# Fused attention and two MoE layers: the beginning split over three DMA queues

## The chip, the cores and the metric

One Trainium2 chip, one of its NeuronCores. The metric is the device time of the program in microseconds, on the slowest core (here the only one); the number given is the median of several executions. Lower is better.

## What is computed

Inputs are float32: q, k and v of 4 batches, 12 heads, 448 positions and 64 channels; two 12 x 12 matrices that mix heads; the weights of two feed-forward layers.

```python
scores = scale * np.matmul(q, k.transpose(0, 1, 3, 2))
scores = np.einsum('bhij,hg->bgij', scores, w_pre)
scores = scores - np.max(scores, axis=-1, keepdims=True)
attn = np.exp(scores)
attn = attn / (np.sum(attn, axis=-1, keepdims=True) + 1e-09)
attn = np.einsum('bhij,hg->bgij', attn, w_post)
x = np.matmul(attn, v)               # then (4*448) x 768 tokens
h = x @ w_in                         # 768 -> 2048, a piecewise quadratic gate, @ w_out
y = softmax-weighted h, layer norm   # 768 -> 1024, * g_ln, @ w_out2
```

## The kernel before, in words

**Order.** The program is not written in the order in which it runs. Every step is a task of a planner (`Order`, L66): an engine, an estimated duration, a priority, the tasks it depends on, and the buffer rings it takes from. `emit` (L100) plays the tasks through on estimated clocks, on each engine always the one that can start first and of those the one with the smallest priority number, and then emits the instructions in that order. So an instruction's place in its engine's queue is fixed by the priorities in `OFFS` (L27) and by estimated durations; on the chip each engine then works through its queue in order and waits where a semaphore tells it to. A DMA is two tasks: the issue, on the engine that issues it, and the transfer, on one estimated DMA server. GpSimd issues through the software queue (q0 in the page), SyncE through the hardware queue (q1).

**Attention.** Work goes through 16 chunks (4 batches x 4 parts of 110 or 118 query rows). A chunk has six qk tasks (`qk`, L297), one for two heads: four 64-row matmuls into two PSUM tiles of the ring `psa` (4 tiles). Each head's scores are evicted to an SBUF tile of the ring `s` (12 tiles; `qk_evac`, L311), on ScalarE, but in the first chunk the odd heads on VectorE. Then a DMA (`remap`, L320) puts them into `sr`: a tile in which a partition is one head and one of ten rows, so that heads lie side by side for mixing. There are two `sr` tiles, used in turn by chunks. Remaps are issued by SyncE, those of the first chunk's odd heads by GpSimd. When all 12 remaps of a chunk have landed, `pre` (L326) mixes heads by matmuls with `wp`, for two tiles of queries at a time (a pair; 90 pairs in all). `rmax` (L335), `expo` (L340), `guard`, `norm` and `wscale` make the softmax and fold its divisor into the second mixing matrix; `post` (L360) mixes again and turns; `evac` (L383) puts the result into `at`, and `av` (L397) multiplies with v. Results go to memory and from there into the two feed-forward layers (`moe`), which run on TensorE until the end.

**The beginning.** `zero_w` (L239) is one GpSimd task: memsets of `wb`, `mk`, `qb`'s padding, `wp` and a strip of `at`. `load_w` (L249), also GpSimd, issues eight small DMAs: the mask four times and the two mixing matrices twice each. `make_w` (L257) multiplies matrices and mask into `wp` and `wk` on VectorE. `zero_s` (L246) sets the four unused rows of each `sr` tile to zero with a VectorE memset, one at the start, one after the first chunk's last eviction (L552). The first chunk's k and q are loaded by SyncE in the pieces listed in `start` (L29): k0, q of pair 0, k1, q of pairs 1 and 2, k2 and k3, q of pairs 3 to 5, k4 and k5 (L524 to L532). The q of every later chunk is one task of two DMAs (L534), whose priority is `sq` below its chunk's first tile; the list `gates` makes such a load wait for a pre matmul where its slot is not negative (L570).

Of the kernel before, what the change touches and what calls it, by code (L numbers as in the profile page):

```python
# [20 lines left out]
HR = 5  # L21
# [5 lines left out]
OFFS = dict(split=-29.45, pre=-0.17, rmax=7.13, expo=-13.24, guard=20.77, norm=-7.75, post=5.7, eh=-57.18, el=-77.04, av0=7.24, avs=1.89, sq=-28.23, exact=174, sld=1000, linact=(), wral=0, early=17, b_in=1000.28, b_x=928.04, b_out=999.37, b_x1=973.79, lw=-90, shal=147, wrp=(), vlp=(),  # L27
   qk0=-14.58, qks=0.45, dmalat=2100, sk=-12.53, sv=3.3, nv=1, svs=0.59,
   mw=-5, start=(('k', 0, 1), ('q', 0, 1), ('k', 1, 1), ('q', 1, 2), ('k', 2, 2), ('q', 3, 3), ('k', 4, 2)))  # L29
# [188 lines left out]
def attention(nc, od, pl, q, k, v, w_pre, w_post, mask, xs):  # L218
# [20 lines left out]
    def zero_w():  # L239
        nc.gpsimd.memset(wb, 0.0)  # L240
        nc.gpsimd.memset(mk, 0.0)
        nc.gpsimd.memset(qb[:, :, :QPAD], 0.0)
        nc.gpsimd.memset(wp, 0.0)
        nc.gpsimd.memset(at[:, :, :, 2 * SEG - R:2 * SEG].rearrange('p k h c -> p (k h) c'), 0.0)

    def zero_s(i):  # L246
        nc.vector.memset(sr[i][0:pad], 0.0)

    def load_w():  # L249
        for i in range(2):  # L250
            for j, w in enumerate((w_pre, w_post)):
                o = 64 * i + (0 if i or j else pad)
                rows = slice(o, o + HR * H)
                nc.gpsimd.dma_start(out=mk[rows, j], in_=mask[:HR, :HR].unsqueeze(1).to_broadcast([HR, H, HR]))
                nc.gpsimd.dma_start(out=wb[rows, j], in_=w.unsqueeze(0).to_broadcast([HR, H, H]))
# [17 lines left out]
    def load_k(b, p):  # L273
        t = pl['kraw'].tile([128, S], F32, tag="kraw", name="kraw")
        nc.sync.dma_start(out=t, in_=k[b, p])
# [180 lines left out]
    t_zs = [add("DVE", 5700, -120, zero_s, 0)]  # L456
    t_lw = add("Pool", 8000, P['lw'], load_w, deps=[t_z], lat=2500)
    t_w = add("DVE", 300, P['mw'], make_w, deps=[t_lw])
# [25 lines left out]
    def make_two(two):  # L484
# [13 lines left out]
        for g, (b, k, pa, pb) in enumerate(groups):  # L498
# [3 lines left out]
            for r in range(2):  # L502
# [3 lines left out]
                    deps=[m] + avs.get(n - 3, []), use=[(r_psb, -2 + r)]))  # L506
# [12 lines left out]
    for i, (b, c) in enumerate(chunks):  # L519
        t0 = t  # L520
        n = GR[c] * R
        if i == 0:
            q0 = {}
            for what, h0, nh in P['start']:  # L524
                if what == 'k':
                    for p in range(h0, h0 + nh):
                        kt[b, p] = od.dma("SP", 450, 640, -100, load_k, b, p, new=[r_kraw])
                else:
                    a1 = od.dma("SP", 1250, nh * 400, -100, load_q, i, b, c, h0, nh,
# [3 lines left out]
        else:  # L533
            a1 = od.dma("SP", 1250, 2000, t0 + P['sq'] - 3, load_q, i, b, c, 0, H // 2, new=[r_q])  # L534
# [588 lines left out]
```

## Time and profile before

| | us |
|---|---|
| median of 3 executions | 1099.97 |
| lowest, highest | 1094.51, 1102.66 |
| the profiled execution | 1098.48 |
| its span, first to last instruction | 1096.7 |
| TensorE busy in it | 1045.8 |
| VectorE, ScalarE, GpSimd busy | 645.6, 553.4, 333.9 |

The profile is of one execution. Busy time is the union of an engine's instructions; on TensorE, where matmuls overlap, a busy stretch is not one at its peak. DMA share is the mean busy share of the core's 16 DMA engines; it can be over 1, since packets overlap. The granted clock is a share of TensorE's full speed.

### The profile page before, as it was taken

The numbers are of one execution on the slowest core, as the hardware profiler recorded it, in microseconds if no ns is written. First come the engines' busy times: TensorE is split into PE (matmuls) and PEld (weight loads), VectorE is DVE, ScalarE is ACT, GpSimd is POOL, SyncE is SP. The second block draws the span as 40 slices with busy tenths as digits, with TensorE's granted clock in tenths as the row PEclk, the third lists the DMA queues.
The fourth block names the chain that finished last, engine by engine and source line by source line (L and its number), as shares of the span: only waits on it lengthen the run. The fifth ranks groups of instructions, "written<-read, shape, count | busy, mean of one in ns | idle before, by whom it ended". The sixth has DMA issues, their size and how long they took to land.

```text
span 1096.7 us, 26955 instructions
## 1 busy us (share of the span) xinstructions
PE 1045.8 (95%) x11200; PEld 866.0 (79%) x11200; DVE 645.6 (59%) x1091; ACT 553.4 (50%) x1201; POOL 333.9 (30%) x438
## 2 busy tenths in 40 slices
PE   6979999999897799999999999999999999999998
PEld 1546666656564699989899998989998899898998
DVE  4445555556457773686869687878766533442242
ACT  3768887788676466433434343343453322333222
POOL 3111111111117854454545455656311000000000
PEclk9999999999999899999999999999999999999999
DMA  8774774775744451423322242424123000000001
GB/s 180 214 198 137 222 213 144 211 225 161 218 149 161 126 181 49 130 81 94 127 82 103 99 142 72 144 101 144 53 79 99 1 30 15 29 15 29 29 15 44
DMA packets 78858, 124.71 MB, mean 114 GB/s; under 512 B 20673, under 2 KB 65825, under 8 KB 78737
## 3 DMA queue, kind: packets, MB, share of 16 engines
q1 hardware_dynamic: 78000, 121.79, 36.7%
q0 software_dynamic: 736, 1.21, 0.6%
q8 instruction: 88, 1.44, 0.6%
q14 instruction: 34, 0.27, 0.1%
HBM read 66.96 MB, written 17.30 MB: 77 GB/s over the span
## 4 chain that ended last, share of the span: by engine, by line
PE 77%; DVE 10%; DMA 4%; ACT 3%; POOL 3%; issue 3%; SPq 0%; ACTq 0%; POOLq 0%; DVEq 0%
PE ps_pre L333 6%; PE ps_h L747 6%; PE ps_h L749 6%; PE ps_h L748 6%; PE ps_o L777 5%; PE ps_o L779 5%; PE ps_qk L306 5%; PE ps_o L778 5%; PE ps_av L420 5%; PE ps_post L369 5%; PE ps_ot L1004 4%; PE ps_ot L1005 4%; PE ps_ot L1003 4%; PE ps_h L943 4%; PE ps_h L945 4%; PE ps_h L944 3%
## 5 line engine op out<-in xcount | busy, mean ns | idle before, releaser
L777 PE MATMUL ps_o<-g,wout 128*128 128x448 f32 x384 | 139.9, 364 | 5.2 <-DVE x2acc L787 5.2
L779 PE MATMUL ps_o<-g,wout 128*128 128x448 f32 x384 | 139.2, 362 | 0.0
L778 PE MATMUL ps_o<-g,wout 128*128 128x448 f32 x384 | 138.8, 362 | 0.0
L369 PEld LDWEIGHTS ps_post<-wr,p 64*64 64x64 f32 x5040 | 101.4, 136 | 47.3 <-issue 29.5
L338 DVE TENSOR_REDUCE nm<-ps_pre 128x1 f32<-128x448 f32 x180 | 105.2, 618 | 48.0 <-PE ps_pre L333 43.7
L343 ACT ACTIVATE p<-ps_pre,nm 128x448 f32<-128x448 f32 x180 | 115.0, 649 | 30.7 <-DVE nm L338 30.6
L666 POOL TENSOR_TENSOR m<-m,v 128x768 f32<-128x768 f32 (+1 forms) x52 | 93.2, 1792 | 80.2 <-DVE v L648 39.5
L787 DVE TENSOR_TENSOR x2acc<-ps_o,x2acc 128x448 f32<-128x448 f32 x168 | 100.4, 617 | 28.1 <-PE ps_o L779 27.8
L369 PE MATMUL ps_post<-wr,p 64*64 64x60 f32 x5040 | 102.0, 221 | 11.3 <-issue 5.5
L769 POOL TENSOR_TENSOR g<-t,g 128x448 fp32r<-128x448 f32 x64 | 89.3, 1399 | 76.4 <-ACT g L765 75.5
L306 PE MATMUL ps_qk<-kraw,qb 64*64 64x448 f32 (+2 forms) x768 | 102.0, 565 | 10.1 <-DMA qb<-in_q_dram 5.3
L333 PE MATMUL ps_pre<-sr,wp 64*64 64x448 f32 (+1 forms) x720 | 99.3, 563 | 9.1 <-DVE at L391 3.5
L317 ACT ACTIVATE s<-ps_qk 119x448 f32<-119x448 f32 (+1 forms) x186 | 92.4, 577 | 29.5 <-PE ps_qk L306 22.1
L350 POOL TENSOR_SCALAR nm<-nm 128x2 f32<-128x2 f32 x90 | 19.1, 212 | 226.4 <-ACT p L343 225.9
L777 PEld LDWEIGHTS ps_o<-g,wout 128*128 128x128 f32 x384 | 72.0, 187 | 13.0 <-DVE x2acc L787 8.6
L638 ACT ACTIVATE v<-v,ebias 128x768 int32<-128x768 int32 (+1 forms) x52 | 46.0, 884 | 66.5 <-DVE v L634 63.2
L779 PEld LDWEIGHTS ps_o<-g,wout 128*128 128x128 f32 x384 | 72.0, 188 | 4.9
L778 PEld LDWEIGHTS ps_o<-g,wout 128*128 128x128 f32 x384 | 72.0, 187 | 4.9
L420 PE MATMUL ps_av<-at,vv 128*64 128x240 f32 (+1 forms) x648 | 72.1, 364 | 3.5 <-issue 3.5
L657 POOL TENSOR_SCALAR m<-m 128x768 f32<-128x768 f32 (+1 forms) x52 | 48.6, 935 | 85.9 <-DVE m L642 59.4
L949 DVE TENSOR_REDUCE st<-ps_h 128x1 f32<-128x1024 f32 x14 | 17.1, 1225 | 96.5 <-PE ps_h L945 96.5
L753 ACT ACTIVATE t<-ps_h,half 128x448 f32<-128x448 f32 x64 | 40.2, 629 | 62.1 <-PE ps_h L749 60.7
(121 smaller groups left out, 2332.2 us busy)
## 6 DMA issues: line engine op xcount, KB each, us to landing
sr<-s SPq DMA_DIRECT2D x138, 192.5 KB
raw<-in_moe_w_out_dram SPq DMA_DIRECT2D x24, 768.0 KB
raw<-in_moe_w_in_dram SPq DMA_DIRECT2D x16, 768.0 KB
sr<-s SPq DMA_DIRECT2D x48, 210.0 KB
raw<-in_moe_w_in_dram SPq DMA_DIRECT2D x12, 512.0 KB
kraw<-in_k_dram SPq DMA_DIRECT2D x24, 224.0 KB
out_dram<-ot SPq DMA_DIRECT2D x13, 384.0 KB
vv<-in_v_dram SPq DMA_DIRECT2D x12, 384.0 KB
```

The source lines that it names most:

```text
L306: nc.tensor.matmul(out=qk_t[b, c, 2 * p + e][64 * j:at_], lhsT=qb[rows, i % 2, lo:hi], rhs=kraw_t[b, p][rows], start=True, stop=True,)
L317: nc.scalar.activation(out=s[:n], in_=qk_t.pop((b, c, h))[:n], func=AF.Copy, scale=0.125)
L333: nc.tensor.matmul(out=pre_t[t][o:o + 64], lhsT=wp[k_], rhs=sr[i % 2][k_, g, :], start=True, stop=True)
L338: nc.vector.tensor_reduce(nm_t[t // 2][:, 0, t % 2:t % 2 + 1], pre_t[t], axis=AX.X, op=ALU.max, negate=True)
L343: nc.scalar.activation(out=p, in_=pre_t.pop(t), func=AF.Exp, bias=nm[:, 0, e], accum_out=nm[:, 1, e])
L369: nc.tensor.matmul(out=ps[i][64 * j:64 * j + 64, k, :], lhsT=ps_p[e][64 * i:64 * i + 64, x:x + 64], rhs=wr[64 * i:64 * i + 64, e], start=T ...
L420: nc.tensor.matmul(out=ps[0][64 * j:64 * j + 64, a, :2 * w].rearrange("p (e s c) -> p e s c", e=2, c=SEG), lhsT=v_t[b][:, 1 + m, h * D:(h ...
L666: nc.gpsimd.tensor_tensor(out=m, in0=m, in1=vt.pop(key).bitcast(F32)[:, :n], op=ALU.mult)
L777: nc.tensor.matmul(out=ps, lhsT=wh, rhs=g[:, 0], start=(i == 0), stop=False)
L778: nc.tensor.matmul(out=ps, lhsT=wh, rhs=g[:, 1], start=False, stop=False)
L779: nc.tensor.matmul(out=ps, lhsT=wl, rhs=g[:, 0], start=False, stop=(i == 1))
L787: nc.vector.tensor_tensor(out=dst, in0=op.pop((u, m)), in1=dst, op=ALU.add)
```

## The change

The planner's offsets are other numbers, for nearly all steps of attention. Of the first chunk's k, the last four are loaded by GpSimd. The strip of `at` gets its own task. The zero rows of `sr` are written by two DMAs that ScalarE issues, from a row that VectorE sets to zero inside `at`. The loads for the first mixing matrix are issued by GpSimd, those for the second by ScalarE. q of the second chunk has a priority of its own, and that of all later chunks at least 1.5, so that the third chunk's waits for the first pair's pre matmuls. Odd heads of the second chunk are evicted by VectorE and remapped by GpSimd, as those of the first chunk are.

```diff
-OFFS = dict(split=-29.45, pre=-0.17, rmax=7.13, expo=-13.24, guard=20.77, norm=-7.75, post=5.7, eh=-57.18, el=-77.04, av0=7.24, avs=1.89, sq=-28.23, exact=174, sld=1000, linact=(), wral=0, early=17, b_in=1000.28, b_x=928.04, b_out=999.37, b_x1=973.79, lw=-90, shal=147, wrp=(), vlp=(),
-   qk0=-14.58, qks=0.45, dmalat=2100, sk=-12.53, sv=3.3, nv=1, svs=0.59,
-   mw=-5, start=(('k', 0, 1), ('q', 0, 1), ('k', 1, 1), ('q', 1, 2), ('k', 2, 2), ('q', 3, 3), ('k', 4, 2)))
+OFFS = dict(split=-55.934, pre=-0.722, rmax=19.723, expo=-9.949, guard=2.949, norm=5.858, post=5.249, eh=-58.542, el=-82.244, av0=7.24, avs=1.895, sq=-29.76, exact=174, sld=1000, linact=(), wral=0, early=17, b_in=1000.28, b_x=928.04, b_out=999.37, b_x1=973.79, lw=-82.042, shal=147, wrp=(), vlp=(),
+   qk0=-14.5, qks=0.45, dmalat=2100, sk=-11.166, sv=2.488, nv=1, svs=0.545,
+   mw=8.068, start=(('k', 0, 1), ('q', 0, 1), ('k', 1, 1), ('q', 1, 2), ('q', 3, 3), ('k', 2, 4)), sq1=-31.946)
...
         nc.gpsimd.memset(mk, 0.0)
+        nc.gpsimd.memset(wp, 0.0)
         nc.gpsimd.memset(qb[:, :, :QPAD], 0.0)
-        nc.gpsimd.memset(wp, 0.0)
+
+    def zero_a():
         nc.gpsimd.memset(at[:, :, :, 2 * SEG - R:2 * SEG].rearrange('p k h c -> p (k h) c'), 0.0)
 
+    z = at[0:pad, 0].rearrange("p h c -> p (h c)")[:, :S]
+
+    def zero_z():
+        nc.vector.memset(z, 0.0)
+
     def zero_s(i):
-        nc.vector.memset(sr[i][0:pad], 0.0)
-
-    def load_w():
+        nc.scalar.dma_start(out=sr[i][0:pad], in_=z.unsqueeze(1).to_broadcast([pad, 12, S]))
+
+    def load_w(j):
+        eng, w = (nc.gpsimd, w_pre) if j == 0 else (nc.scalar, w_post)
         for i in range(2):
-            for j, w in enumerate((w_pre, w_post)):
-                o = 64 * i + (0 if i or j else pad)
-                rows = slice(o, o + HR * H)
-                nc.gpsimd.dma_start(out=mk[rows, j], in_=mask[:HR, :HR].unsqueeze(1).to_broadcast([HR, H, HR]))
-                nc.gpsimd.dma_start(out=wb[rows, j], in_=w.unsqueeze(0).to_broadcast([HR, H, H]))
+            o = 64 * i + (0 if i or j else pad)
+            rows = slice(o, o + HR * H)
+            eng.dma_start(out=mk[rows, j], in_=mask[:HR, :HR].unsqueeze(1).to_broadcast([HR, H, HR]))
+            eng.dma_start(out=wb[rows, j], in_=w.unsqueeze(0).to_broadcast([HR, H, H]))
...
-    def load_k(b, p):
+    def load_k(b, p, eng="SP"):
         t = pl['kraw'].tile([128, S], F32, tag="kraw", name="kraw")
-        nc.sync.dma_start(out=t, in_=k[b, p])
+        (nc.gpsimd if eng == "Pool" else nc.sync).dma_start(out=t, in_=k[b, p])
...
-    t_zs = [add("DVE", 5700, -120, zero_s, 0)]
-    t_lw = add("Pool", 8000, P['lw'], load_w, deps=[t_z], lat=2500)
-    t_w = add("DVE", 300, P['mw'], make_w, deps=[t_lw])
+    t_zz = add("DVE", 400, -120, zero_z)
+    t_zs = [od.dma("Activation", 500, 250, -115, zero_s, j, deps=[t_zz]) for j in range(2)]
+    t_za = add("Pool", 1300, -5, zero_a)
+    t_lw = [od.dma("Pool", 2400, 100, P['lw'], load_w, 0, deps=[t_z]), od.dma("Activation", 2000, 100, -118, load_w, 1, deps=[t_z])]
+    t_w = add("DVE", 300, P['mw'], make_w, deps=t_lw)
...
-                    deps=[m] + avs.get(n - 3, []), use=[(r_psb, -2 + r)]))
+                    deps=[m, t_za] + avs.get(n - 3, []), use=[(r_psb, -2 + r)]))
...
-                        kt[b, p] = od.dma("SP", 450, 640, -100, load_k, b, p, new=[r_kraw])
+                        en = "SP" if p < 2 else "Pool"
+                        kt[b, p] = od.dma(en, 600 if p > 1 else 450, 640, -100 + p, load_k, b, p, en, new=[r_kraw])
                 else:
-                    a1 = od.dma("SP", 1250, nh * 400, -100, load_q, i, b, c, h0, nh,
+                    a1 = od.dma("SP", 1250, nh * 400, -100 + h0, load_q, i, b, c, h0, nh,
...
-            a1 = od.dma("SP", 1250, 2000, t0 + P['sq'] - 3, load_q, i, b, c, 0, H // 2, new=[r_q])
-            gates.append((a1, t0 + P['sq'] - 3))
+            pr = P['sq1'] if i == 1 else max(t0 + P["sq"] - 3, 1.5)
+            a1 = od.dma("SP", 1250, 2000, pr, load_q, i, b, c, 0, H // 2, new=[r_q])
+            gates.append((a1, pr))
...
-            first = i == 0 and h % 2
+            first = i < 2 and h % 2
...
-            en, dur = ("Pool", 1000) if first else ("SP", 850)
-            rms.append(od.dma(en, dur, 900, pr, remap, i, b, c, h, en, deps=[a2], use=[(r_s, -1)],
+            en, dur = ("Pool", 600) if first else ("SP", 850)
+            rms.append(od.dma(en, dur, 600 if first else 900, pr, remap, i, b, c, h, en, deps=[a2], use=[(r_s, -1)],
                               new=[] if h else [r_sr], join=[r_sr] if h else []))
-        if i == 0:
-            t_zs.append(add("DVE", 5700, -10, zero_s, 1, deps=[a2]))
```

## Rows read from the trace of the kernel before

**Rows 1.** The page, part 1: engine, busy us, share, instructions.

```profile
PE 1045.8 (95%) x11200; PEld 866.0 (79%) x11200; DVE 645.6 (59%) x1091; ACT 553.4 (50%) x1201; POOL 333.9 (30%) x438
```

**Rows 2.** Busy time by stretch: length, then each engine; clock, DMA share, GB/s.

```profile
105.00:285.00 180.00, 172.68 (x4214) 112.36 (x4206) 99.95 (x232) 148.35 (x408) 29.46 (x102) 1.00 0.68 195
...
385.00:1097.00 712.00, 702.17 (x3571) 648.77 (x3567) 428.34 (x654) 278.99 (x480) 233.27 (x215) 1.00 0.23 76
```

**Rows 3.** The same for ps_pre alone: PE, PEld, DVE, ACT; clock, DMA, GB/s.

```profile
0.00:27.00 27.00, 0.00 (x0) 0.00 (x0) 0.00 (x0) 0.00 (x0) 0.96 0.85 179
27.00:105.00 78.00, 25.47 (x168) 8.82 (x168) 24.56 (x42) 27.84 (x81) 0.95 0.70 187
105.00:285.00 180.00, 53.36 (x408) 16.59 (x408) 59.72 (x102) 73.95 (x208) 1.00 0.68 195
```

**Rows 4.** The chain that ended last, 0 to 40 us: start, us, what.

```profile
11.34 12.78 DMA sr<-s
...
28.06 2.99 PE ps_pre L333 x16
```

**Rows 5.** Busy time by stretch of the start (columns as in rows 2).

```profile
1.00:10.00 9.00, 6.30 (x26) 1.68 (x28) 5.83 (x4) 2.19 (x4) 6.76 (x12) 1.00 0.75 176
10.00:22.00 12.00, 7.60 (x52) 2.02 (x48) 7.26 (x7) 3.98 (x8) 2.38 (x4) 1.00 1.06 194
13.00:25.00 12.00, 6.64 (x46) 2.06 (x48) 5.82 (x5) 4.08 (x9) 1.31 (x3) 0.98 0.95 193
25.00:31.00 6.00, 6.00 (x32) 3.26 (x34) 1.16 (x2) 3.46 (x9) 0.00 (x0) 0.50 0.69 185
```

**Rows 6.** Tile sr, 0 to 24 us: ns min/median/max, starts; landing of GpSimd's issues.

```profile
L322 POOL DMA_DIRECT2D sr<-s x6: 590/600/607, 7.5 to 15.2; - x6
...
DMA to landing us min/median/max: 7.3/10.3/11.3
```

**Rows 7.** Timeline of SyncE's DMA issues: start, us, what.

```profile
4.42 1.07 SPq L275 DMA_DIRECT2D kraw<-in_k_dram  x2
...
6.83 1.07 SPq L275 DMA_DIRECT2D kraw<-in_k_dram  x2
...
9.36 6.18 SPq L322 DMA_DIRECT2D sr<-s  x6
15.70 1.68 SPq L282 DMA_DIRECT2D qb<-in_q_dram  x2
18.51 14.17 SPq L322 DMA_DIRECT2D sr<-s  x11
```

**Rows 8.** Timeline of 0 to 32 us, other engines.

```profile
0.72 1.28 ACT L317 ACT_TABLE_LOAD   x1 [0.72 <-PEq L1107]
...
1.90 4.54 DVE L247 MEMSET sr<- 4x5376 f32 x1 [1.90 <-issue]
...
5.48 0.54 ACT L317 ACTIVATE s<-ps_qk 119x448 f32<-119x448 f32 x1 [3.48 <-PE ps_qk L306]
...
5.94 0.61 POOL L255 DMA_DIRECT2D wb<-in_w_post_dram  x1
...
6.53 0.62 DVE L315 TENSOR_SCALAR s<-ps_qk 119x448 f32<-119x448 f32 x1
...
7.45 0.61 POOL L322 DMA_DIRECT2D sr<-s  x1 [0.90 <-DVE s L315]
...
11.60 0.62 DVE L315 TENSOR_SCALAR s<-ps_qk 119x448 f32<-119x448 f32 x1 [1.02 <-PE ps_qk L306]
...
14.81 0.21 DVE L258 TENSOR_TENSOR wp<-wb,mk 128x60 f32<-128x60 f32 x1
...
16.21 4.54 DVE L247 MEMSET sr<- 4x5376 f32 x1 [1.05 <-issue]
```

**Rows 9.** DMA issues, 0 to 24 us: count, KB each, median us to landing.

```profile
kraw<-in_k_dram SPq DMA_DIRECT2D x6, 224.0 KB
sr<-s POOLq DMA_DIRECT2D x6, 192.5 KB, 10.3
qb<-in_q_dram SPq DMA_DIRECT2D x4, 165.0 KB
...
wb<-in_w_post_dram POOLq DMA_DIRECT2D x2, 2.8 KB, 3.2
```

**Rows 10.** Waits of TensorE, 80 to 400 us: total, times, longest, us.

```profile
PE ps_av L411 <- DVE t L761: 4.4, 1, 4.4
```

## The prediction

> **What bounds the kernel now.** The page comes first [rows 1]: TensorE is busy for 1045.8 us, 95% of the span, so time is won where it stands still or runs slowly. The table by stage [rows 2] shows where the change can reach: the reader compares TensorE's busy time with the length of each stretch. From 105 to 285 us it is busy for 172.68 of 180 us; all that the diff rewrites as code lies in the first 30 us, and the rest of attention is touched through priorities alone. The same view narrowed to the pre matmuls [rows 3] gives the pace: none before 27 us; 168 of them, which is 21 pairs of tiles at 8 a pair, in the next 78 us, or 3.71 us a pair; then 408, or 51 pairs, in 180 us, 3.53 us a pair. So attention begins late, and for its first quarter it runs 21 x (3.71 - 3.53), nearly 3.9 us, behind its own later pace.
>
> Why is the first pair late? The chain of waits [rows 4] leads through a remap transfer that was issued at 11.34 us and landed 12.78 us later, and from it over the last qk matmuls to the pre matmuls. The stages [rows 5] show what those 12.78 us are: between 10 and 22 us the DMA share is 1.06 at 194 GB/s; remaps stand behind other transfers, not behind instructions. The six that GpSimd issued took 7.3 to 11.3 us to land [rows 6], the same saturation seen from the other queue. Before that, in 1 to 10 us, the share is only 0.75. After it, in 25 to 31 us, the granted clock is 0.50, the lower of the two levels (1.2 instead of 2.4 GHz), after 12 us in which TensorE was busy for 6.64.
>
> **The change part by part.** I make the sum against the profiled execution (1098.48 us, span 1096.7) and carry the difference to the median shown, 1099.97; the two are 0.14% apart.
>
> *Loads of k2 to k5 by GpSimd.* SyncE issued them in the two stretches of 1.07 us from 4.42 and 6.83 us, and its first remap went out at 9.36 us [rows 7], although the first head was evicted at 5.48 + 0.54 = 6.02 [rows 8]. Without them SyncE is free 2.1 us earlier, near 7.2. GpSimd starts its four loads after the small memsets, near 1 us, at some 0.6 us each like its remaps [rows 6]. What that is worth is the DMA time that stands empty: against a full share of 1.05 the 9 us from 1 to 10 lack 0.30, so 2.7 us of full DMA. It can be filled only from the time at which GpSimd's first load reaches memory, and part of it is issue time of the small q pieces, which stay. Bounds 0 and 2.7; I take 1.3, half.
>
> *q of the third chunk, moved behind the first pair.* Its two transfers of 165 KB go out at 15.70 us [rows 7, 9], ahead of all remaps of the second chunk and beside the tail of those of the first. 330 KB at 194 GB/s are 1.7 us of DMA. On SyncE's own queue they stand behind the first chunk's remaps, so they take from these only where queues share engines. Bounds 0 and 1.7; I take 0.9. They come back after the first pair, where the third chunk's qk needs them and the share, 0.69, has room.
>
> *Zero rows by DMA in place of two memsets.* The two memsets of 4.54 us leave VectorE [rows 8]. The second (from 16.21 us) hid under the remaps, in a stretch in which VectorE had nothing else; the first ended at 6.44 and the first odd eviction began at 6.53, against 5.48 on ScalarE, so it comes about 1 us earlier, but what it feeds is not last: the transfers are. I cost both at nothing gained. What is added is 2 x 4 rows of 12 x 448 words, 172 KB: 0.9 us at 194 GB/s if it meets full engines, nothing if it fits into the room before 10 us. I take a loss of 0.4.
>
> The Trainium skill (DMA: Bandwidth & Descriptors, "Why a DMA increments its semaphore by 16 and not by 1") says that a transfer is spread over the largest number of engines, up to 16, that divides both outermost sizes, on the hardware queues the lowest-numbered ones. By it the four zero rows would run on 4 engines, among those that the remaps of ten partitions use, and my estimate from it is four times the 0.9 us on these; the sum would be some 3 us lower. No row here shows single DMA engines.
>
> *Weights split over two queues.* Four of the eight small issues, which ended at 6.55 us on GpSimd [rows 8], move to ScalarE, beside two zero-row issues. VectorE's first instruction starts at 1.90 us, so the zero source is there near 2.4; six issues at 0.6 us (GpSimd's) to 1.03 (SyncE's six remaps in 6.18 us, waits included [rows 7]) are 3.6 to 6.2 us, so ScalarE's first eviction starts at 6.0 to 8.6 us instead of 5.48. If the table load of 1.28 us, now done by 2.00, is put behind them, 1.3 later still. The cover: SyncE cannot send the first remap before 7.2 us anyway, and the engines are full afterwards. Without that cover it costs the difference, up to 3 us; I take 0.
>
> *Odd heads of the second chunk to VectorE and GpSimd.* Six evictions of some 0.54 us leave ScalarE and are some 0.6 us on VectorE; six remaps leave SyncE's queue, where eleven took 14.17 us [rows 7]. VectorE has only the memset in that stretch, which goes away. The bytes are the same. The second chunk can be complete sooner, which helps the stretch to 105 us: of the 3.9 us behind pace I take 1.5 back; bounds 3.9 and, if remaps on GpSimd's queue land too late for the sixth pair, -2, half of it the other way.
>
> *Clock.* 6 us at 0.50 with TensorE busy throughout [rows 5] would be 3.0 us less at full clock. With the matmuls closer together some of it comes back: bounds 0 and 3.0; I take 1.0, since the waits for remaps remain between them.
>
> *New priorities over all of attention* (row maxima and normalisation later, exponentials later against evictions of scores, loads of k one or two tiles later). No row shows the new order. The longest single wait of TensorE between 80 and 400 us is 4.4 us [rows 10]: one such wait gone or one added bounds it at 4.4 either way; I take 0.
>
> Sum: 1.3 + 0.9 - 0.4 + 1.5 + 1.0 = 4.3 us less. 1098.48 becomes 1094.2 for a profiled execution, and the median of 1099.97 becomes **1095.7 us**. What comes after attention follows TensorE (702.17 of 712 us busy after 385 us [rows 2]) and should only move forward.
>
> **The rivals.**
>
> *A. The whole start is given back.* All terms at their upper ends: 2.7 + 1.7 - 0.4 + 3.9 + 3.0 = 10.9 us, 1089.1. For it: the waits hang together, earlier remaps make denser matmuls and so no fall of the clock. Against it: 12 remaps of 192.5 KB [rows 9] still have to pass a DMA that is full from 10 to 22 us.
>
> *B. The transfers are the bound and stay so.* More queues put the same bytes into full engines; the first pair still starts past 27 us, q comes back behind it, and only the zero rows are new: 1099.97 + 0.4, so 1099 to 1101. For it: the share of 1.06, and remaps that land no sooner from GpSimd's queue than from SyncE's. Against it: the empty DMA time before 10 us. The Trainium skill (DMA: Bandwidth & Descriptors, "Issuing engines are not separate DMA queues") states just this: transfers of all issuers share the same 16 DMA engines, and several issuers save only issue time. The trace agrees for 10 to 22 us, where two queues together moved 194 GB/s.
>
> *C. Slower: VectorE stands still for the mixing weights.* make_w ran at 14.81 us, after the last odd eviction, when the weights were long there (issued until 6.55, landing after some 3 us) [rows 8, 9]. Now half of them stand behind four k loads, 896 KB, on GpSimd's queue. That queue moved six remaps, 1155 KB, from 7.45 to about 15.2 + 11 us, some 62 KB per us [rows 6, 8]; at this rate the k loads end near 15.5 us and the weights near 16. If make_w is put among VectorE's odd evictions, those behind it (from 11.60 us on) wait until 16: 4.4 us, and with them their PSUM buffers, their remaps and the first pair; the gains ahead of that don't show. 1099.97 + 4.4 = 1104.4. It decides as soon as make_w stands before the fourth odd eviction and the weights land after 12 us. Against it: these loads start before SyncE has filled the engines, and could land at twice that rate.
>
> *D. The change doesn't do what it says*: the new order moves a wait to a later stretch, worth 4.4 either way beside the 4.3: 1091.3 or 1100.1.
>
> **How the numbers follow.** The forecast's case 0.48, A 0.18, B 0.17, C 0.08, D 0.09. About 1% (11 us) is what a measurement of this kernel tells from no change. Below 1089.0 lie two thirds of A (0.12), a tenth of the forecast's case (0.05), a third of D (0.03), and 0.05 for A or the forecast together with an order that gains: 0.25. Above 1111 needs C together with an order that loses, or a waiting queue that I have not seen: 0.07. The rest, 0.68, is within 1%. The range goes from 1085 (A with most of D's gain) to 1104 (C).
>
> **What would show it.** Right: the first pre matmul at 24 to 26 us; a DMA share near 1 from 4 us on; a granted clock over 0.50 in the 6 us around the first pair; 21 pairs done near 101 us and all later stages 4 us earlier. Wrong: a first pre still past 27 us with full DMA engines (B); a wait of VectorE for mask or weight transfers ahead of make_w (C); TensorE's idle time between 105 and 385 us different by more than 4 us (D); a start that is earlier and an end that is not, because attention's tail waits for something of its own.

## The result, and the profile after

The changed kernel takes 1110.63 us (median of 21 executions, 1097.85 to 1118.15); the kernel before, run beside it, 1100.54 (21, 1090.81 to 1108.31). The ratio is 1.0109, with a 95% interval of 1.0084 to 1.0134: slower by 1.1%, some 12 us, where 4.3 us less were forecast. All ratios here compare fast executions alone and so differ from the quotient of the two medians, which is 1.0092 here. The profiled execution took 1118.15 us, the top of its range, and 19.7 us more than the profiled execution of the kernel before, so its stages show more lost than the median has.

The page of the kernel after, part 1, answers to [rows 1]:

```profile
PE 1053.8 (94%) x11200; PEld 871.1 (78%) x11200; DVE 639.4 (57%) x1096; ACT 550.5 (49%) x1195; POOL 337.6 (30%) x444
```

TensorE does the same 11200 matmuls. The stages that answer to [rows 2] (length, then each engine's busy time; clock, DMA share, GB/s):

```profile
105.00:285.00 180.00, 172.90 (x4067) 110.95 (x4066) 96.72 (x223) 142.33 (x393) 28.41 (x98) 0.98 0.67 190
```

TensorE is as busy from 105 to 285 us as before, but with 4067 matmuls in place of 4214: it works on an earlier part of the program. The pre matmuls alone, as in [rows 3]:

```profile
27.00:105.00 78.00, 23.27 (x144) 7.25 (x144) 20.97 (x36) 23.73 (x69) 0.89 0.75 177
105.00:285.00 180.00, 54.66 (x399) 16.62 (x400) 57.38 (x98) 70.87 (x200) 0.98 0.67 190
```

144 instead of 168 by 105 us: three pairs fewer, 10.6 us at 3.53 us a pair. That is about half of the 19.7 us. It is lost in the beginning, where [rows 5] stood:

```profile
1.00:10.00 9.00, 3.50 (x8) 0.58 (x8) 0.48 (x2) 0.00 (x0) 4.78 (x9) 1.00 0.88 186
10.00:22.00 12.00, 8.78 (x42) 3.87 (x46) 3.20 (x7) 3.79 (x6) 1.45 (x3) 1.00 0.46 89
22.00:31.00 9.00, 4.49 (x34) 1.31 (x31) 1.87 (x3) 2.25 (x5) 3.60 (x7) 0.88 0.87 190
31.00:45.00 14.00, 10.54 (x119) 3.53 (x114) 7.66 (x16) 6.88 (x20) 4.66 (x12) 0.83 0.92 165
```

The second line is the one to read. From 10 to 22 us the DMA share is 0.46 and 89 GB/s, where it was 1.06 and 194: the stretch that was full of transfers is now half empty, so not the transfers are late but their issues. ScalarE's timeline (start, us, what; ACTq is its DMA issue) shows one place:

```profile
1.34 1.27 ACTq L254 DMA_DIRECT2D sr<-at  x1
8.06 0.82 ACTq L261 DMA_DIRECT2D mk<-in_mask_dram  x1
10.89 0.76 ACTq L262 DMA_DIRECT2D wb<-in_w_post_dram  x1
13.10 0.72 ACTq L261 DMA_DIRECT2D mk<-in_mask_dram  x1
13.86 0.73 ACTq L262 DMA_DIRECT2D wb<-in_w_post_dram  x1
14.63 0.70 ACTq L254 DMA_DIRECT2D sr<-at  x1
15.36 1.28 ACT L324 ACT_TABLE_LOAD   x1 [15.36 <-DMA mk<-in_mask_dram]
16.66 1.42 ACT L324 ACTIVATE s<-ps_qk 119x448 f32<-119x448 f32 x3
```

Six issues take 5.00 us by their durations (1.27 + 0.82 + 0.76 + 0.72 + 0.73 + 0.70) but last from 1.34 to 15.33: they wait. The first eviction begins at 16.66 us, in place of 5.48 [rows 8]. What they wait for stands in the built program: ScalarE and SyncE take turns on eight completion semaphores (DMAHW0 to 7), and an issue that takes one again waits until the transfer that had it has landed.

```
L254 DMA sr<-at      [waits DVE]
L261 DMA mk<-mask    [waits DMAHW3, Pool]
L262 DMA wb<-w_post  [waits DMAHW4]
L261 DMA mk<-mask    [waits DMAHW5]
L262 DMA wb<-w_post  [waits DMAHW6]
L254 DMA sr<-at      [waits DMAHW7]
L324 ACT_TABLE_LOAD
```

GpSimd's timeline shows the other place:

```profile
5.56 0.60 POOL L262 DMA_DIRECT2D wb<-in_w_pre_dram  x1
20.55 0.83 POOL L246 MEMSET at<- 128x840 f32 x1 [14.39 <-DMA sr<-at]
21.32 3.55 POOL L329 DMA_DIRECT2D sr<-s  x6
```

Before the change the strip's memset was in GpSimd's first microsecond. Now it comes after the two zero-row transfers, which read their zeros from `at`, and it writes `at`; so it waits 14.39 us for the second of them, the last of ScalarE's six issues. The two waits are one chain: that issue went out only at 14.63. Behind it stand the six remaps of the odd heads, which went out from 7.45 to 15.20 us before [rows 6, 8] and now leave together at 21.32. The waits of the first 60 us (engine, line, released by: total, times, longest, us) name both, each with one long wait:

```profile
ACT L324 <- DMA mk<-in_mask_dram: 15.4, 1, 15.4
...
POOL at L246 <- DMA sr<-at: 14.4, 1, 14.4
```

SyncE's timeline, as in [rows 7], and the end of the chain in that stretch, as in [rows 4]:

```profile
3.06 6.10 SPq L289 DMA_DIRECT2D qb<-in_q_dram  x6
17.23 20.10 SPq L329 DMA_DIRECT2D sr<-s  x12
...
43.37 8.38 SPq L289 DMA_DIRECT2D qb<-in_q_dram  x4
```

```profile
26.78 16.53 DMA sr<-s
...
43.37 13.11 DMA qb<-in_q_dram
...
56.53 2.18 PE ps_qk L313 x7
```

The first remap of SyncE goes out at 17.23, not at 9.36. The first pre matmuls begin at 36.81 (27.50 before, by TensorE's timelines), and q of the third chunk, now behind them, is issued at 43.37 and lands 13.11 us later; its first qk runs at 56.53.

### The profile page after: what moved, and what is told of

Same layout as the page of the kernel before. It is cut to its first block, busy times and chain, and to the rows that moved or that the text cites. A ratio compares the mean times of both kernels' runs of the same rounds, so it can differ in the third digit from the quotient of the medians.

```text
span 1116.4 us, 26967 instructions
## 1 busy us (share of the span) xinstructions
PE 1053.8 (94%) x11200; PEld 871.1 (78%) x11200; DVE 639.4 (57%) x1096; ACT 550.5 (49%) x1195; POOL 337.6 (30%) x444
## 4 chain that ended last, share of the span: by engine, by line
PE 76%; DVE 9%; DMA 7%; ACT 3%; issue 2%; POOL 2%; SPq 0%; ACTq 0%; POOLq 0%; DVEq 0%
PE ps_qk L313 6%; PE ps_h L756 6%; PE ps_h L758 6%; PE ps_h L757 6%; PE ps_pre L340 5%; PE ps_o L786 5%; PE ps_o L788 5%; PE ps_o L787 5%; PE ps_post L376 5%; PE ps_av L427 5%; PE ps_ot L1013 4%; PE ps_ot L1014 4%; PE ps_ot L1012 3%; PE ps_h L952 3%; PE ps_h L954 3%; PE ps_h L953 3%
## 5 line engine op out<-in xcount | busy, mean ns | idle before, releaser
L376 PEld LDWEIGHTS ps_post<-wr,p 64*64 64x64 f32 x5040 | 106.1, 138 | 43.7 <-issue 23.7
L340 PE MATMUL ps_pre<-sr,wp 64*64 64x448 f32 x720 | 105.4, 575 | 20.0 <-DMA sr<-s 6.1
L313 PE MATMUL ps_qk<-kraw,qb 64*64 64x448 f32 (+2 forms) x768 | 104.1, 593 | 16.6 <-DVE s L322 6.8
L376 PE MATMUL ps_post<-wr,p 64*64 64x60 f32 x5040 | 105.3, 223 | 8.0 <-ACT p L350 3.1
L324 ACT ACTIVATE s<-ps_qk 119x448 f32<-119x448 f32 (+1 forms) x180 | 88.9, 578 | 21.9 <-PE ps_qk L313 20.8
L340 PEld LDWEIGHTS ps_pre<-sr,wp 64*64 64x64 f32 (+1 forms) x720 | 31.4, 137 | 66.0 <-issue 24.3
```

Of the source, the lines that this page charges most:

```text
L313: nc.tensor.matmul(out=qk_t[b, c, 2 * p + e][64 * j:at_], lhsT=qb[rows, i % 2, lo:hi], rhs=kraw_t[b, p][rows], start=True, stop=True,)
L340: nc.tensor.matmul(out=pre_t[t][o:o + 64], lhsT=wp[k_], rhs=sr[i % 2][k_, g, :], start=True, stop=True)
L376: nc.tensor.matmul(out=ps[i][64 * j:64 * j + 64, k, :], lhsT=ps_p[e][64 * i:64 * i + 64, x:x + 64], rhs=wr[64 * i:64 * i + 64, e], start=T ...
```

## The experiments

The theory after this reading: the price are the two waiting queues, ScalarE's (its evictions start 11 us late) and GpSimd's (the remaps behind the strip). Rivals: the late q, the k loads on GpSimd's queue, the odd heads, the priorities. Every ratio is to the kernel before on the same chip; a point is 1% of its time, 11 us. e5 and e13 have 6 executions, the others 10 to 21. The two columns of times are from the timelines of GpSimd (first remap) and ScalarE (first eviction), one profiled execution each. The kernels "only ScalarE's issues" also hold the new offsets of make_w and of the weight loads, and those with k2 to k5 by GpSimd the new order of SyncE's first loads.

| run | what differs from before | GpSimd | ScalarE | ratio, 95% |
|---|---|---|---|---|
| after | everything | 21.3 | 16.7 | 1.0109, 1.0084 to 1.0134 |
| e1 | after, strip zeroed first | 8.0 | 16.1 | 1.0051, 1.0019 to 1.0084 |
| e2 | after, all weights by GpSimd | 17.3 | 10.0 | 1.0111, 1.0075 to 1.0148 |
| e3 | after, q as before | 21.0 | 16.3 | 1.0111, 1.0074 to 1.0148 |
| e5 | after, old priorities | 21.3 | 16.6 | 1.0111, 1.0054 to 1.0167 |
| e13 | only ScalarE's issues, strip waiting | 20.1 | 14.7 | 1.0103, 1.0052 to 1.0154 |
| e9 | only ScalarE's issues, strip later | 10.2 | 15.6 | 1.0052, 1.0013 to 1.0091 |
| e8 | only ScalarE's issues, strip early | 6.7 | 16.6 | 1.0028, 0.9994 to 1.0061 |
| e4 | only new priorities | 7.3 | 5.4 | 1.0047, 1.0016 to 1.0077 |
| e10 | after without both waits | 8.7 | 5.6 | 1.0048, 1.0016 to 1.0081 |
| e16 | e1, q as before | 7.8 | 16.2 | 1.0051, 1.0015 to 1.0087 |
| e18 | e10, q as before | 8.7 | 5.6 | 1.0055, 1.0019 to 1.0092 |
| e6 | only k by GpSimd | 10.1 | 5.4 | 0.9977, 0.9936 to 1.0018 |
| e7 | only odd heads | 7.4 | 5.5 | 1.0000, 0.9968 to 1.0032 |
| e12 | only k4, k5 by GpSimd | 8.0 | 5.5 | 1.0026, 0.9999 to 1.0053 |
| e14 | e12 and odd heads | 7.9 | 5.4 | 0.9991, 0.9958 to 1.0025 |
| e15 | only q late | 7.4 | 5.7 | 0.9971, 0.9935 to 1.0006 |
| e17 | k by GpSimd and q late | 11.2 | 5.5 | 1.0022, 0.9982 to 1.0061 |
| e11 | k by GpSimd, q late, odd heads | 8.7 | 6.1 | 1.0027, 1.0001 to 1.0053 |

**Parts taken out of the changed kernel.** e1 zeroes the strip ahead of everything that reads from `at`:

```diff
         nc.gpsimd.memset(qb[:, :, :QPAD], 0.0)
+        nc.gpsimd.memset(at[:, :, :, 2 * SEG - R:2 * SEG].rearrange('p k h c -> p (k h) c'), 0.0)
 
     def zero_a():
-        nc.gpsimd.memset(at[:, :, :, 2 * SEG - R:2 * SEG].rearrange('p k h c -> p (k h) c'), 0.0)
+        pass
```

> Edit: the memset of the strip of at stands with GpSimd's other memsets at the start, so GpSimd waits for no zero-row transfer before its odd remaps; all else as in the changed kernel. Theory of the queues (each engine's start-up work waits in line behind DMA issues or memsets that wait for transfers): GpSimd's first odd remap goes out near 10 us instead of 21.3, ScalarE's first eviction stays near 16.7 us; the first pre matmul comes at 31 to 34 us instead of 36.8, and the ratio to the kernel before falls from 1.011 to about 1.006. Rival (the DMA engines are the bound, the order of issue does not matter): first pre near 36 us and 1.011.

GpSimd's timeline of e1, where most remaps go as soon as VectorE has their scores:

```profile
8.03 0.61 POOL L330 DMA_DIRECT2D sr<-s  x1 [1.55 <-DVE s L323]
16.10 0.60 POOL L330 DMA_DIRECT2D sr<-s  x1 [7.46 <-DVE s L323]
18.59 0.59 POOL L330 DMA_DIRECT2D sr<-s  x1 [1.89 <-DVE wk L272]
```

The first pre is no earlier (37.0 us), and yet the ratio falls by 0.58 points, more than half of the loss, by one line of code. This pair alone doesn't settle it: the two intervals meet at 1.0084, and the quotient of e1's medians, 1104.08 by 1095.12, is 1.0082. Three more pairs follow.

e2 issues all eight weight loads from GpSimd, behind the k loads:

```diff
     def load_w(j):
-        eng, w = (nc.gpsimd, w_pre) if j == 0 else (nc.scalar, w_post)
+        if j:
+            return
         for i in range(2):
+            for j, w in enumerate((w_pre, w_post)):
...
```

> Edit: all eight mask and weight loads are issued by GpSimd behind its k loads; ScalarE issues only the two zero-row transfers. Theory of the queues: ScalarE's first eviction comes at 7 to 9 us instead of 16.7, GpSimd's strip no longer waits beyond 12 us, first pre near 28 to 30 us, ratio about 1.002; VectorE's make_w, which stands before the fourth odd eviction, may then wait for the weights until 15 us (rival C of the prediction), which would put the first pre at 31 to 33. Rival (new priorities cost the time): first pre earlier by as much, but the ratio stays at 1.008 or more.

ScalarE's first eviction is at 10.00 now, 6.7 us earlier than in the changed kernel, and the first pre at 33.4; but the strip's memset runs at 16.56, the remaps from 17.33, and the ratio stays at 1.0111, where about 1.002 was expected. To relieve ScalarE alone is worth nothing that shows.

e3 gives q its old rule, e5 the priorities of attention their old values (diff shortened):

```diff
-            pr = P['sq1'] if i == 1 else max(t0 + P["sq"] - 3, 1.5)
+            pr = P['sq1'] if i == 1 else t0 + P["sq"] - 3
```

```diff
-OFFS = dict(split=-55.934, pre=-0.722, rmax=19.723, expo=-9.949, guard=2.949, norm=5.858,
...
+OFFS = dict(split=-29.45, pre=-0.17, rmax=7.13, expo=-13.24, guard=20.77, norm=-7.75,
...
```

> Edit: q of the third chunk has its old priority rule and no wait for the first pair; all else as in the changed kernel. Theory of the queues: the wait for q at 43 to 56 us goes, the third chunk's qk starts 8 to 12 us earlier than 56.5, first pre unchanged near 37, and the ratio falls by 0.003 to 0.005. Rival (only the first pair's delay counts, everything behind it is caught up): no change, 1.011.

> Edit: the changed kernel with the old offsets, except those of the weight loads, of make_w, of the list of first loads and of the second chunk's q: the new beginning alone. Two-part theory (beginning and priorities each cost about half of the 11 us): ratio 1.004 to 1.008, first pre at 35 to 38 us. Rival (the beginning costs everything, the 1.0047 of the priorities alone is chance): 1.010 or more.

Both 1.0111. In e3 the third chunk's qk came at 36.8 us, 20 us earlier than in the changed kernel, for nothing. While the strip waits, neither q's old place nor the old priorities take away a part of the loss that shows (e5, with 6 executions, leaves 1.0054 to 1.0167).

**Parts put alone into the kernel before.** e4 takes the new priorities, e6 the k loads, e7 the odd heads of the second chunk:

```diff
-OFFS = dict(split=-29.45, pre=-0.17, rmax=7.13, expo=-13.24, guard=20.77, norm=-7.75,
...
+OFFS = dict(split=-55.934, pre=-0.722, rmax=19.723, expo=-9.949, guard=2.949, norm=5.858,
...
```

> Edit: the kernel before with the new offsets (all but those of the weight loads, of make_w and of the list of first loads, and without the wait of the third chunk's q). Theory of the queues: 1.000 to 1.003, first pre near 27.5 us. Rival (the priorities cost the time): 1.008 to 1.011 with a first pre near 27.5 us.

```diff
-        nc.sync.dma_start(out=t, in_=k[b, p])
+        (nc.gpsimd if eng == "Pool" else nc.sync).dma_start(out=t, in_=k[b, p])
...
+                        en = "SP" if p < 2 else "Pool"
```

> Edit: the kernel before with k2 to k5 loaded by GpSimd ahead of the weights and the new order of SyncE's first loads; all else old. Theory of the queues: k2 lands near 13 us instead of 8, because four loads on a second queue take DMA time from the pieces that are needed first; the qk of heads 4 and 5 starts near 13 us, and GpSimd's first odd remap waits behind weight loads that wait for the k loads, until 12 us or later; first pre at 31 to 34 us instead of 27.5, ratio 1.002 to 1.006. Rival (the prediction: loads sent sooner fill empty DMA time): first pre at 25 to 27 us, ratio 0.998 or less.

```diff
-            first = i == 0 and h % 2
+            first = i < 2 and h % 2
```

> Edit: the kernel before with the odd heads of the second chunk evicted by VectorE and remapped by GpSimd; all else old. Theory of the queues (and the prediction): a free move, first pre 26 to 28 us, ratio 0.997 to 1.000. Rival (the moved heads land late on GpSimd's queue and hold VectorE): 1.002 or more.

e4 is slower by 0.47%, 5 us, between what its theory and its rival had; e6 and e7 are no change. TensorE's timeline of e6 shows what the k loads hold back:

```profile
3.64 3.26 PE L306 MATMUL ps_qk<-kraw,qb 64*64 64x448 f32 x8 [3.64 <-DMA qb<-in_q_dram]
9.86 11.70 PE L306 MATMUL ps_qk<-kraw,qb 64*64 64x448 f32 x80 [2.95 <-DMA qb<-in_q_dram]
```

SyncE's first remap does go out at 7.12 us, 2.2 us earlier; but with GpSimd's four loads beside them the second pair waits for its q until 9.86. The DMA share from 1 to 10 us does rise, from 0.75 [rows 5] to 0.89, but what comes sooner isn't what is needed first, and the first pre comes at 28.21 in place of 27.50. e12 leaves k2 and k3 on SyncE:

```diff
...
+                        en = "SP" if p < 4 else "Pool"
...
```

> Edit: the kernel before with only k4 and k5 loaded by GpSimd (k4 ahead of the weights, k5 behind them), so that k0 to k3 keep their turn on SyncE's queue; all else old. Theory of the queues: no q or k piece that is needed first is delayed, SyncE's first remap goes out near 8 us, first pre at 25 to 27 us, ratio 0.994 to 0.999. Rival (the DMA engines are the bound): 1.000, first pre at 27.5.

1.0026: no better, with a first pre at 32.9 us where 25 to 27 were expected. e8 issues zero rows and second weights from ScalarE, with the strip zeroed early:

```diff
     def zero_s(i):
-        nc.vector.memset(sr[i][0:pad], 0.0)
+        nc.scalar.dma_start(out=sr[i][0:pad], in_=z.unsqueeze(1).to_broadcast([pad, 12, S]))
...
+        eng, w = (nc.gpsimd, w_pre) if j == 0 else (nc.scalar, w_post)
```

> Edit: the kernel before with the zero rows and the second matrix's loads issued by ScalarE (the strip of at in its own task, which here stands ahead of GpSimd's first load and waits only for VectorE's first memset); all else old. Theory of the queues: the six issues wait for transfers that SyncE issued before them, ScalarE's first eviction starts at 10 to 15 us instead of 5.5, first pre at 31 to 34 us, ratio 1.003 to 1.007. Rival (the prediction: covered, evictions by 8.6 us at the latest, first pre near 27.5): 1.000.

ScalarE's timeline is that of the changed kernel from the issue at 13.10 us on, table load and evictions included:

```profile
15.35 1.28 ACT L324 ACT_TABLE_LOAD   x1 [15.35 <-DMA mk<-in_mask_dram]
16.64 1.42 ACT L324 ACTIVATE s<-ps_qk 119x448 f32<-119x448 f32 x3
```

The first pre is at 32.8, 5.3 us late, and the ratio is 1.0028 with an interval that holds 1. e9 was to add the strip's wait, by zeroing it behind GpSimd's weight loads:

```diff
...
+        if j == 0:
+            nc.gpsimd.memset(at[:, :, :, 2 * SEG - R:2 * SEG].rearrange('p k h c -> p (k h) c'), 0.0)
...
```

> Edit: the kernel before with the zero rows and the second matrix's loads issued by ScalarE, as in the run with ScalarE's DMA issues alone, and with the memset of the strip of at behind GpSimd's four weight loads, where it waits for the zero-row transfers that read there; all else old. Theory of the queues: GpSimd's first odd remap goes out near 21 us instead of 6.7 in that run, first pre at 35 to 37 us instead of 32.8, ratio 1.006 to 1.010: the two waits together are the loss. Rival (the strip's wait is covered by ScalarE's late evictions): as in that run, first pre near 33 us and 1.003.

It missed its aim: there the memset waited for the first zero-row transfer alone and ran at 7.22. e13 puts it directly ahead of the first odd remap:

```diff
         n = GR[c] * HR
+        if (i, h) == (0, 1):
+            nc.gpsimd.memset(at[:, :, :, 2 * SEG - R:2 * SEG].rearrange('p k h c -> p (k h) c'), 0.0)
         (nc.gpsimd if eng == "Pool" else nc.sync).dma_start(
```

> The kernel before with zero rows and second weights issued by ScalarE (as in e8), and the strip's memset put directly ahead of GpSimd's first remap, so that it waits for both zero-row transfers. Theory, the waiting queues: the strip runs at about 20 us, GpSimd's remaps start behind it at 20 to 21 instead of 6.7, the first pre matmul comes at 35 to 37 us (32.8 in e8), and the ratio is 1.006 to 1.010. Rival, the strip's wait is covered by ScalarE's: ratio 1.003 as in e8, first pre matmul near 33 us.

GpSimd's timeline of e13, and the same of e8, whose code differs in that memset's place alone:

```profile
19.35 0.83 POOL L330 MEMSET at<- 128x840 f32 x1 [15.28 <-DMA sr<-at]
20.12 3.57 POOL L331 DMA_DIRECT2D sr<-s  x6
```

```profile
1.36 0.83 POOL L246 MEMSET at<- 128x840 f32 x1 [0.35 <-DVE at L251]
...
6.69 0.61 POOL L329 DMA_DIRECT2D sr<-s  x1 [2.00 <-DVE s L322]
12.99 0.61 POOL L329 DMA_DIRECT2D sr<-s  x1 [5.69 <-DVE s L322]
```

1.0103, against 1.0028, although ScalarE's first eviction is 1.9 us earlier than in e8. With the old priorities of attention, the old q, the old k and the old odd heads, ScalarE's issues and the waiting strip give a loss as large as the whole one of the changed kernel (6 executions, 1.0052 to 1.0154). The first pre, however, is at 33.8 us in its profile and not at 35 to 37.

**Combinations.** e10 is the changed kernel without either wait: strip first, zero rows by VectorE as before, all weights by GpSimd between k2 and k3. e11 is the kernel before with k by GpSimd, odd heads and the late q, so e10 with the old priorities.

```diff
     def zero_s(i):
-        nc.scalar.dma_start(out=sr[i][0:pad], in_=z.unsqueeze(1).to_broadcast([pad, 12, S]))
+        nc.vector.memset(sr[i][0:pad], 0.0)
...
-    t_lw = [od.dma("Pool", 2400, 100, P['lw'], load_w, 0, deps=[t_z]), od.dma("Activation", 2000, 100, -118, load_w, 1, deps=[t_z])]
+    t_lw = [od.dma("Pool", 4800, 100, P['lw'], load_w, 0, deps=[t_z])]
```

> Edit: the changed kernel without what makes the queues wait: the strip stands in front, all weight loads are issued by GpSimd between its load of k2 and those of k3 to k5, the zero rows are memsets of VectorE as before; k loads, odd heads, the wait of the third chunk's q and the new priorities stay. Theory of the queues: first pre at 27 to 30 us, ratio 0.998 to 1.003. Rival (something else of the change costs the time: k on GpSimd's queue, the moved q or the priorities): 1.006 or more.

```diff
+            pr = -31.946 if i == 1 else max(t0 + P["sq"] - 3, 1.5)
...
+                        en = "SP" if p < 2 else "Pool"
...
-            first = i == 0 and h % 2
+            first = i < 2 and h % 2
```

> Edit: the kernel before with k2 to k5 loaded by GpSimd (weights between k2 and k3), the odd heads of the second chunk moved and the new rule for the q loads; zero rows, weights and priorities as before. Theory of the queues: 0.995 to 1.000, first pre at 26 to 28 us. Rival (the moved q costs 5 us or more where the third chunk waits for it): 1.003 or more.

1.0048 and 1.0027. The loss has halved, but in e10 it is not gone, although the first pre is at 28.6. Whether the late q is the rest was asked of four runs. e15 puts q's rule alone into the kernel before (the first line of e11's diff), e16 takes it out of e1, e18 out of e10 (both as e3's diff):

> The kernel before with only q's new priority rule: q of the third and all later chunks at 1.5 or later. Theory, q's late place costs by itself: third chunk's qk at 42 to 48 us instead of 30.5, ratio 1.002 to 1.004. Rival, it is covered by the second chunk's work and the pace of the pairs: ratio 0.999 to 1.001.

> e1 (the changed kernel with the strip zeroed first, 1.0051; ScalarE still starts its evictions at 16 us) with q of the third chunk loaded as early as before. Theory, q's late place hides what ScalarE's late start costs, or costs it itself: ratio 1.001 to 1.003. Rival, ScalarE's late start and the priorities are the price: ratio 1.004 to 1.006, first pre matmul at 37 us or later.

> e10 (the changed kernel without the waits in both queues, 1.0048, new priorities) with q of the third and later chunks loaded as early as before; e14 held another kernel than its expectation says (the kernel before with k4, k5 by GpSimd and the odd heads moved, all priorities and q as before), so this question is still open. Theory, the new priorities are what is left of the loss in e10: ratio 1.003 to 1.006. Rival, q's late place is: third chunk's qk at 30 to 40 us instead of 48.7, ratio 0.999 to 1.002. If ScalarE's late start is a price of its own, the ratio lies below that of e16 (1.0051), which differs from this kernel in ScalarE's issues and the zero rows and weights alone.

q's place is not it: alone 0.9971, taken out of e1 no change (1.0051), taken out of e10 no gain (1.0055, with the third chunk's qk at 36.2 us in place of 48.7). e16 and e18 differ in what ScalarE issues: first evictions at 16.2 and 5.6 us, and the same ratio. So ScalarE's late start, the most striking line of the profile, has no price of its own here that these runs can tell; by the two intervals, up to 0.5 points either way would not show. The expectation of e14 speaks of e10, by a mistake: the kernel that ran is the kernel before with k4 and k5 by GpSimd (e12's diff) and the odd heads moved (e7's), and it is read as that. e18 is the run that the expectation describes.

> e10 (the changed kernel without the waits in both queues, 1.0048) with q of the third chunk loaded as early as before. Theory, q's late place is what is left of the loss there: third chunk's qk at 30 to 37 us instead of 48.7, ratio 1.000 to 1.002. Rival, the other priorities are what is left: third chunk's qk earlier all the same, ratio 1.004 to 1.006.

0.9991: the odd heads on top of e12 cost nothing. Last, e17 joined the two parts whose ratios lay just under 1:

```diff
...
+                        en = "SP" if p < 2 else "Pool"
...
+            pr = -31.946 if i == 1 else max(t0 + P["sq"] - 3, 1.5)
...
```

> The kernel before with two harmless parts of the change together: k2 to k5 by GpSimd (0.9977 alone in e6) and q of the third and later chunks late (0.9971 alone in e15). If both were small gains and add up: ratio 0.993 to 0.996, a version that beats both kernels, first pre matmul at 26 to 28 us. If they are no change and scatter about 1: 0.998 to 1.003.

1.0022: they don't add up to a gain. No version here is faster than the kernel before by more than its interval.

**What the table says.** The five kernels whose GpSimd sends its first remap after 17 us, because the strip's memset waits, give 1.0103 to 1.0111, whatever else they hold. The fourteen that send it by 11.2 us give 0.9971 to 1.0055. Four pairs differ in that wait: after and e1, e3 and e16, e13 and e8, and e2 and e10, where the way of the zero rows differs too. They give 0.58, 0.60, 0.75 and 0.63 points, each give or take 0.4 to 0.6 by its two intervals; together that is about 0.6, give or take 0.25. The quotients of medians give the same four as 0.10, 0.92, 0.70 and 0.41. So that the wait costs is shown by the four together; how much is known to within 4 to 10 us.

What makes the rest is less sure. Among the fourteen, the five with the new priorities give 1.0047 to 1.0055, and the nine with the old ones 0.9971 to 1.0028, but for e9 with 1.0052, which stays unexplained (its remaps start 3.5 us later than those of e8). e8 and e9, the two of the nine in which ScalarE issues, have the two highest ratios, so that beside the old priorities a price of ScalarE's late start, 0.3 to 0.5 points, is not ruled out. Nor is it settled whether the prices add: with the strip waiting, old and new priorities give 1.0111 and 1.0109, but the difference is known only to 0.6 points. The granted clock does not sort the kernels: its mean over a run's executions is 0.9848 in e14 (ratio 0.9991) and 0.9895 in e3 (1.0111).

Where in attention the losses are paid is open as well. The pre matmuls from 20 to 130 us, first of the kernel after, then of e13 and of e4 (columns as in [rows 3]):

```profile
20.00:130.00 110.00, 31.71 (x208) 9.97 (x208) 29.17 (x50) 34.28 (x100) 0.92 0.74 182
```

```profile
20.00:130.00 110.00, 31.82 (x224) 10.96 (x224) 31.41 (x55) 37.40 (x108) 0.95 0.72 192
```

```profile
20.00:130.00 110.00, 31.87 (x232) 10.19 (x232) 32.48 (x56) 38.71 (x112) 0.97 0.75 192
```

The same view of the kernel before counts 232. The changed kernel is three pairs or 10.6 us behind at 130 us, and its last pre matmul starts at 377.5 us, some 20 us after that of the kernel before (357.6). So all that its profiled execution lost is lost within attention, but only about half of it by 130 us. The count doesn't follow the ratio from kernel to kernel either: e1, at half the loss, has 208 as well. e13 is one pair, 3.5 us, behind, and its profiled execution, the fastest of its 6, is 3.5 us longer than the profiled one of the kernel before (1101.95 and 1098.48); what its slower executions lose, no trace shows. e4 is not behind at 130 us, and its profiled execution is 5.1 us longer (1103.55), so what that one lost came later. One profiled execution a kernel, with executions of the kernel before spread from 1086 to 1110 us, can't place the losses closer. That the strip's wait costs is shown; by which way the wait, and the new priorities, reach the end stays open.

## Why the prediction was wrong

**The step that failed** is "Zero rows by DMA in place of two memsets". It priced the change by its bytes, 0.4 us with bounds 0 and 0.9, and the two memsets that go away at nothing. It didn't ask which instruction has to wait for the new transfers. Their source lies inside `at`, the strip that is to be zeroed lies in `at` too, and the strip's new task comes after them. The memset waits 14.39 us on GpSimd, and what is queued behind it, the odd remaps, waits with it. The four pairs of kernels with and without the wait show the size: about 0.6 points, 4 to 10 us, in place of 0.4 us. The signs of it are in the diff: a task moved from the head of a queue to a later place, and a shared tile.

The Trainium skill (PSUM — Partial Sum Buffer, "Engine vs sequencer instructions") states that the queues of ScalarE, VectorE and GpSimd are strictly first in, first out. The trace agrees: VectorE had evicted the first odd head by 10.44 us (9.82 + 0.62), and its remap left GpSimd at 21.32, behind the memset.

**Weights split over two queues**: the issue times were right (six issues of 0.70 to 1.27 us), but the step took them back to back and put ScalarE's first eviction at 6.0 to 8.6 us; it came at 16.66, since each of the last five issues waits for the semaphore of a transfer that SyncE issued. The table load went behind them, as the step allowed. Its price of 0 held all the same within what these runs can tell: e16 and e18 are equal, and e8 (1.0028) has an interval that reaches from no cost to 0.6%. That was luck: the cover which it named, a first remap of SyncE no sooner than 7.2 us and full engines afterwards, was not there. That remap went out at 17.23 us, and the DMA share from 10 to 22 us was 0.46.

**New priorities**: taken as 0, with 4.4 us as the bound on either side. e4 gives 0.47%, 5 us, with an interval from 1.8 to 8.5 us, and e10, e16 and e18, which hold other parts too, lie near it. Measured alone, that is the second term that was mis-sized; whether its bound was too narrow the interval doesn't tell. In the changed kernel itself, taking the new priorities out gave nothing back that shows (e5). Which waits the new order moved was not read.

**The terms that were to gain** gave nothing that can be measured. k by GpSimd: SyncE is free at 7.12, as the step said (7.2), but q lands later (e6). Odd heads: a free move (e7, e14), where 1.5 us were to come back. q of the third chunk: no gain, no loss (e15), though in the changed kernel its transfers took 13.11 us once they were issued. The clock gave nothing back: 0.83 from 31 to 45 us, between the two levels of 1.2 and 2.4 GHz, with TensorE waiting in between, and a mean of 0.93 over the first 50 us in both kernels.

**The rivals.** A didn't come. B had the engines full: they stood at 0.46. The sentence behind B (the Trainium skill, DMA: Bandwidth & Descriptors, "Issuing engines are not separate DMA queues") states that several issuers save issue time alone. The runs agree that there is no more to gain: not one of the splits gained. The issue time itself was not saved on ScalarE, whose six issues lasted from 1.34 to 15.33 us. C named the right kind of event, an engine in order whose first instruction waits for a DMA, with VectorE and make_w in that part; make_w did stand ahead of the fourth odd eviction, and the last of its weight loads was issued only at 13.86 us, but the third odd eviction, ahead of it, began at 17.60 for another reason (its matmul), and make_w ran right behind that, at 18.14, as VectorE's timeline shows:

```profile
17.60 0.62 DVE L322 TENSOR_SCALAR s<-ps_qk 119x448 f32<-119x448 f32 x1 [1.86 <-PE ps_qk L313]
18.14 0.21 DVE L265 TENSOR_TENSOR wp<-wb,mk 128x60 f32<-128x60 f32 x1
```

The queue that the experiments point to was GpSimd's: the "waiting queue that I have not seen". The prediction gave it, and C with a worse order, 0.07 together for a time above 1111 us; the median of 1110.63 lies just below that. Of the signs named, "a start that is earlier" and "full DMA engines" were both wrong; the low DMA share together with a late first pre was on no list.

## What to carry to other kernels

When work is moved to a DMA, ask first what its source is and who writes that tile next: here the write waited 14.39 us for the transfer that read it, and everything behind it on that engine's queue waited too. Look at the waits that DMA issues on a compute engine may carry, and not at their duration alone: six issues of 5.00 us lasted 14. And a long wait in the profile is not yet a cost: here two stood side by side with nearly the same length, and only the experiments told that relieving one (e2) gives nothing back that shows, and taking away the other about half of the loss.

## What was not expected

- In this program the DMA issues of SyncE and ScalarE are tied together by the eight semaphores that they share. ScalarE's second issue stood until 8.06 us and its last until 14.63, for transfers that SyncE had issued; their own durations add up to 5.00 us.
- ScalarE's table load is not done at the start as such. It ran at 0.72 us where an eviction was ScalarE's first work [rows 8], and at 15.36 where DMA issues stood ahead.
- A first eviction 11 us later (e16 against e18, to within 0.5 points) and a first pre some 9 us later (36.9 us in e14, ratio 0.9991) cost nothing measurable: the time of the first pair, by which the prediction steered, is a poor measure of this kernel's end.
